# Sixteen more pairs in the layout of four chains, their values inside the y products

## The chip, the core and the metric

One core of a Trainium2 chip runs the whole program. The metric is the device time of one execution in microseconds. TensorE (PE in the rows) does the matmuls, VectorE (DVE) and ScalarE (ACT) the element-wise work and everything that leaves PSUM, GpSimd (POOL) some sums, SyncE (SP) issues the loads and stores.

## What is computed

The reference is windowed attention on 8 batches x 8 heads x 576 tokens x 64, followed by a feed-forward layer with a parametric ReLU on all 4608 tokens. Four heads of a batch see the last 32 tokens ("plain"), four see every fourth of the last 128 ("dilated").

```
scores = scale * np.matmul(q, k.transpose(0, 1, 3, 2))
mask_plain = (rel >= 0) & (rel < window)
mask_dil = (rel >= 0) & (rel < window * dilation) & (rel % dilation == 0)
...
attn = np.exp(scores)
attn = attn / (np.sum(attn, axis=-1, keepdims=True) + 1e-09)
return np.matmul(attn, v).astype(np.float32)
...
h = x @ w_in
g = np.maximum(h, 0.0) + alpha * np.minimum(h, 0.0)
return (g @ w_out).astype(np.float32)
```

x is the attention's output, 4608 x 512; w_in is 512 x 2048.

## The kernel before

Attention is done in 32 *pairs* of heads (8 batches x 4; class Pair; pair 4b + c). A dilated head is sorted by residue first, so that both kinds have a band of blocks: 32 queries against 64 keys. The steps of a pair are `scores` (PE; 36 small matmuls into two PSUM banks, each done as two passes, so 72 in the trace), `maxima` (DVE, four operations: mask and maximum), `exponentials` (ACT, nine), `divisions` (DVE, three), `turns` (DVE, one transpose of the probabilities from pr to pt), `values` (PE, from pt and v into PSUM tiles o), and `highs` and `lows`, which copy o to where the feed-forward layer or a store takes it. `keep` stores it.

Each large product is done as three passes on 128 x 128 weights and 512 columns (high x high, high x low, low x high). The work runs in 48 *slices*: slice n is one block f of 128 of the 2048 hidden units for one tile t of 512 tokens, tiles 0, 1 and 2. In slice n stand `ffn_h` of slice n + 1 (12 matmuls of 512 columns), the parametric ReLU (either `ffn_relu` on ACT and `ffn_sum` on DVE, or `ffn_parts`, two operations on DVE, in the slice after scores), `ffn_high` (ACT) and `ffn_low` (DVE), which split g in two parts, and `ffn_y` of slice n - 1 (12 matmuls into four y banks, column block by column block). Beside them stand preparations for the next stage: `combined_low` (wc) and `others_low` (ysum) on DVE with sums on GpSimd, and from slice 39 on parts of the next tiles. After the slices comes the *paired stage*, which does six tiles two at a time.

Pairs 0 to 7 stand at the start. Pairs 8 to 23 stand in slices 17 to 46. Pairs 24 to 31 stand in the paired stage, and these use the *layout of four chains* (`mixed`): a head is cut in chains of 5, 5, 4 and 4 blocks (`CHAINS`) in place of two halves of 9, v is laid out to fit (vX in place of vW), and the mask is another one. Values are then 42 matmuls on four o tiles, one for a chain; in the layout of halves 38 on two.

Every engine works in the order in which the code issues. PSUM has eight banks: four y banks, and four a banks that go round in turn (`bank("a", ...)`): each ffn_h takes the next one, scores of pairs 8 to 23 the next two, values the next two. A tile in a bank can be written when the reader of the bank's last tile is done.

`score_at`, `value_at` and `divide_at` say in which slice scores, values and divisions stand. Before, the values of a pair stand in the slice of the next pair's scores, right behind them. pr and pt exist once, so turns of a pair comes behind the values of the pair before it.

Of the kernel before, what the change touches and what calls it, by code (L numbers as in the profile page):

```python
# [66 lines left out]
def tile_window_attention_prelu_ffn(  # L67
# [127 lines left out]
    class Pair:  # L195
        def __init__(self, b, c):
            self.b, self.c = b, c
            p = b * NC + c
            self.onto = p <= NC + 1
            self.banks = "y" if self.onto else "a"  # L200
            self.late = p == 0
            self.plain = 2 * c < HP
            self.mask = PLAIN if self.plain else DILATED
            self.id = f"{b}_{c}"
            self.pr = spare_pr[p % 2] if b < 2 else pr0
            self.room = rooms[c] if b < 2 else None
            self.sm = sums[p % 2]
            self.mixed = p >= AHEAD
            self.kept = {}

        def target(self, t):

            if t not in KEPT:
                return half(t, self.c)
            if t not in self.kept:
                if self.mixed:
# [4 lines left out]
            return self.kept[t][0]  # L221

# [4 lines left out]
        def load_qk(self):  # L227
            b, c = self.b, self.c
            if self.mixed:
                self.k, self.q = lasting("k")[:, :S], lasting("q")[:, :S]  # L230
            elif self.room is None:
                self.k = att.tile([P, S], F32, tag="k", name=f"k_{self.id}")
                self.q = att.tile([P, S], F32, tag="q", name=f"q_{self.id}")
            else:
                self.k, self.q = self.room[:, :S], self.room[:, S:2 * S]
            nc.sync.dma_start(out=self.k, in_=kT[b, c])
            nc.sync.dma_start(out=self.q, in_=qT[b, c])

        def load_v(self):
            if self.mixed:  # L240
# [5 lines left out]
            nc.sync.dma_start(out=self.v, in_=vX[self.b - AHEAD // NC, self.c] if self.mixed else vW[self.b, self.c])  # L246

        def scores(self):


            if self.mixed:
# [91 lines left out]
        def turns(self):  # L343

            self.pt = lasting("pt") if self.mixed else att.tile([P, HB * BK], F32, tag="pt", name=f"pt_{self.id}")
            nc.vector.transpose(self.pt, self.pr.rearrange("q j k -> q (j k)"))
# [19 lines left out]
        def places(self):  # L366

            base = self.b * S
            if self.mixed:
                for n, (first, length) in enumerate(CHAINS):  # L370
                    a, last = first * BQ, (first + length) * BQ
                    flat = self.po[n].rearrange("d i q -> d (i q)")
                    while a < last:
                        if self.plain:
                            t = (base + a) // TT
                            z = min(last, (t + 1) * TT - base)
                            to = self.target(t)[:, base + a - t * TT:base + z - t * TT]
                        else:
# [4 lines left out]
                            to = self.target(t).rearrange("d (i r) -> d r i", r=DILATION)[:, r, i:i + z - a]  # L383
                        yield n % 2, flat[:, a - first * BQ:z - first * BQ], [to]
# [26 lines left out]
        def highs(self):  # L411
# [5 lines left out]
        def lows(self, copy=nc.vector.tensor_copy):  # L417
            for u, src, to in self.out:
                if len(to) == 2:
                    nc.vector.tensor_tensor(out=to[1], in0=src, in1=to[0].bitcast(F32), op=ALU.subtract)  # L420
                elif u == 1:
                    copy(out=to[0], in_=src)
# [105 lines left out]
    def ffn_y(t, f):  # L528
# [10 lines left out]
        for c in range(NC):  # L539
            for n, (a, e) in enumerate(PASSES):  # L540
# [3 lines left out]
                )  # L544

# [647 lines left out]
    def masks_of(kind):  # L1193
        nc.sync.dma_start(out=mask_sb[:, kind:kind + HB], in_=masks[:, kind:kind + HB])
# [97 lines left out]
    for n in range(CUT):  # L1292
# [16 lines left out]
        if scored:  # L1309
            scored.maxima()  # L1310
            if n == 0:
                behind(scored.nm, load, pairs[7].load_qk, pairs[7].load_v, lambda: masks_of(PLAIN))
# [42 lines left out]
    for n in range(CUT, NS):  # L1355
# [36 lines left out]
        if SECOND - 2 <= n < NS - 1:  # L1392
# [5 lines left out]
            ffn_high(*slices[n + 1])  # L1398
            if divided:
# [3 lines left out]
        if not whole:  # L1403
            ffn_y(*slices[n - 1])
# [7 lines left out]
        if valued:  # L1412
            valued.values()
            pairs[pairs.index(valued) + 1].load_v()
# [7 lines left out]
        if valued:  # L1422
            valued.highs()
            put[n + 1].append(valued.keep)
        if scored:
            scored.exponentials(5)
        if valued:
            valued.lows(nc.scalar.copy)
# [5 lines left out]
        if n == HALF + 1:  # L1434
            pairs[2 * NC].load_qk()
            pairs[2 * NC].load_v()
        if n in combine_at:
# [9 lines left out]
        if n == NS - 2:  # L1447
            nc.sync.dma_start(out=mask_sb, in_=masks[:, NMASK:2 * NMASK])
# [80 lines left out]
```

## Time and profile before

| | |
|---|---|
| median of 3 runs | 847.58 us (845.1 to 848.56) |
| profiled execution | 847.35 us |
| its span, first to last instruction | 845.6 us |
| PE busy | 825.9 us (98%) |
| DVE busy | 652.3 us (77%) |
| ACT busy | 466.3 us (55%) |
| granted TensorE clock | 0.996 of 2.4 GHz |

Busy times are sums over an engine's instructions with overlaps counted once; the difference of execution and span lies before the first and after the last instruction.

### The profile page before, as it was taken

Reading aid. Unit: us, or ns where it says so; the run is one execution under the profiler, and the core shown is the slowest. Engines: PE = TensorE matmul, PEld = TensorE weight load, DVE = VectorE, ACT = ScalarE, POOL = GpSimd, SP = SyncE. Lnnn points to the kernel's source line nnn. Section 1 sums busy time; section 2 is a strip of 40 time slices with the busy share of each in tenths; the row PEclk is TensorE's granted clock in tenths of the full one; section 3 lists DMA queues with packets and bytes.
Section 4 is the critical chain, followed back from the end, with each engine's and each line's share of the span. In section 5 each row is a group of like instructions: output and inputs, shape, how many; then the busy total and the mean of one; then the engine's idle time right before and its main releaser. Section 6 shows DMA issues by size and latency. Waiting matters only on the chain.

```text
span 845.6 us, 20392 instructions
## 1 busy us (share of the span) xinstructions
PE 825.9 (98%) x8014; PEld 671.3 (79%) x8014; DVE 652.3 (77%) x1087; ACT 466.3 (55%) x1276; POOL 87.0 (10%) x88
## 2 busy tenths in 40 slices
PE   8889999999999999999999999999999999999998
PEld 5677888878887887887888788878887888888886
DVE  5887767777668689879966999897289988944983
ACT  7785766735444555667436752665176436624640
POOL 0000000115575454000000000000000000000000
PEclk9999999999999999999999999999999999999999
DMA  7843389769776768595899599866876886666664
GB/s 255 277 160 126 125 255 276 250 210 280 250 251 222 266 213 286 193 302 168 266 311 303 156 326 298 260 183 201 252 208 196 288 286 198 192 194 190 197 191 157
DMA packets 131485, 194.90 MB, mean 230 GB/s; under 512 B 11582, under 2 KB 67518, under 8 KB 131390
## 3 DMA queue, kind: packets, MB, share of 16 engines
q1 hardware_dynamic: 131390, 193.60, 71.9%
q8 instruction: 63, 1.03, 0.5%
q14 instruction: 32, 0.26, 0.1%
HBM read 145.33 MB, written 48.23 MB: 229 GB/s over the span
## 4 chain that ended last, share of the span: by engine, by line
PE 81%; DVE 10%; ACT 4%; issue 2%; DMA 1%; SPq 0%; DVEq 0%; ACTq 0%
PE h L495 15%; PE qA L1027 15%; PE y L541 14%; PE pA L726 11%; PE qC L1027 7%; PE pC L726 6%; PE qB L1027 4%; PE o L361 3%; PE pB L726 3%; PE s L266 2%; DVE held L785 1%; ACT pr L331 1%; DVE stage L778 1%; DVE gp L840 1%; DVE py L956 1%
## 5 line engine op out<-in xcount | busy, mean ns | idle before, releaser
L495 PE MATMUL h<-x,w_dt.float32r 128*128 128x512 f32 x576 | 145.2, 401 | 3.3 <-DVE pr L318 1.2
L541 PE MATMUL y<-g,w_dt.float32r 128*128 128x512 f32 x576 | 138.3, 389 | 0.7 <-DVE ob L549 0.7
L495 PEld LDWEIGHTS h<-x,w_dt.float32r 128*128 128x128 f32 x576 | 108.6, 192 | 27.6 <-DVE pr L318 1.6
L541 PEld LDWEIGHTS y<-g,w_dt.float32r 128*128 128x128 f32 x576 | 108.0, 188 | 23.5 <-issue 1.1
L331 ACT ACTIVATE pr<-pr,nm 128x64 f32<-128x64 f32 x216 | 72.4, 338 | 25.7 <-DVE nm L321 25.4
L771 ACT COPY stage<-pA 128x512 f32<-128x512 f32 x72 | 42.2, 586 | 47.4 <-PE pA L726 46.5
L726 PE MATMUL pA<-parts_w,ring_w 128*128 128x512 f32 x234 | 58.2, 391 | 0.2 <-ACT stage L771 0.2
L835 ACT CAST gp<-held 128x512 fp32r<-128x512 f32 x60 | 37.2, 620 | 35.6 <-DVE held L831 35.4
L726 PE MATMUL pA<-parts_w,ring_xA 128*128 128x512 f32 x222 | 55.4, 393 | 0.7 <-ACT stage L771 0.7
L503 ACT ACTIVATE m<-h 128x512 f32<-128x512 f32 x33 | 19.7, 598 | 60.4 <-PE h L495 50.1
L726 PEld LDWEIGHTS pA<-parts_w,ring_w 128*128 128x128 f32 x234 | 43.6, 188 | 9.8 <-ACT stage L771 0.6
L526 DVE TENSOR_TENSOR g<-m,g 128x512 fp32r<-128x512 f32 x48 | 37.9, 789 | 15.5 <-ACT g L521 15.5
L726 PEld LDWEIGHTS pA<-parts_w,ring_xA 128*128 128x128 f32 x222 | 41.2, 188 | 10.5 <-ACT stage L771 1.9
L521 ACT CAST g<-m 128x512 fp32r<-128x512 f32 x48 | 29.7, 618 | 35.6 <-DVE m L508 18.1
L778 DVE TENSOR_TENSOR stage<-pC,stage 128x512 f32<-128x512 f32 x48 | 33.0, 688 | 13.4 <-ACT stage L771 8.3
L952 ACT COPY py<-qA 128x512 f32<-128x512 f32 x24 | 13.8, 588 | 52.0 <-PE qA L1027 51.2
L1027 PE MATMUL qA<-gp,ring_xA 128*128 128x512 f32 x174 | 42.3, 390 | 0.0
L840 DVE TENSOR_TENSOR gp<-held,gp 128x512 fp32r<-128x512 f32 x60 | 40.7, 686 | 1.6 <-ACT gp L835 1.6
L331 ACT ACTIVATION_READ_ACCUMULATOR pr<-pr,nm 128x1 f32 x216 | 40.9, 189 | 0.0
L956 DVE TENSOR_TENSOR py<-qC,py 128x512 f32<-128x512 f32 x24 | 16.0, 688 | 31.0 <-PE qC L1027 24.7
L1027 PE MATMUL qA<-gp,ring_w 128*128 128x512 f32 x162 | 39.5, 389 | 0.0
L1027 PEld LDWEIGHTS qA<-gp,ring_xA 128*128 128x128 f32 x174 | 32.5, 188 | 7.0 <-DVE gp L840 0.2
(188 smaller groups left out, 1702.7 us busy)
## 6 DMA issues: line engine op xcount, KB each, us to landing
ring_w<-wS SPq DMA_DIRECT2D x69, 256.0 KB, 3.2
ring_xA<-wS SPq DMA_DIRECT2D x66, 256.0 KB, 2.9
ring_xA<-wY SPq DMA_DIRECT2D x40, 256.0 KB, 3.8
ring_w<-wY SPq DMA_DIRECT2D x36, 256.0 KB, 3.5
ring_g<-wS SPq DMA_DIRECT2D x33, 256.0 KB, 3.0
wO<-w_dt.float32r SPq DMA_DIRECT2D x32, 256.0 KB, 4.3
wS<-wc SPq DMA_DIRECT2D x16, 512.0 KB, 4.3
ring_w<-wO SPq DMA_DIRECT2D x31, 256.0 KB, 3.3
```

Source lines behind the costliest of these rows:

```text
L331: nc.scalar.activation(out=self.pr[:, r, :], in_=self.ps[r // CUT0][:, r % CUT0, :] if self.onto else self.pr[:, r, :], func=AF.Exp, bias= ...
L361: nc.tensor.matmul(self.po[u][e * D:(e + 1) * D, a:z, :], lhsT=self.v[rows, i, :], rhs=self.pt[rows, a * BK + (BQ if i else 0):z * BK - (B ...
L495: nc.tensor.matmul(ms[t, f], lhsT=weight(0, a, f)[:, c * P:(c + 1) * P], rhs=half(t, c)[:, e, :], start=(c == 0 and n == 0), stop=(c == NC ...
L521: nc.scalar.copy(out=g[:, 0, :], in_=ms[t, f])
L526: nc.vector.tensor_tensor(out=g[:, 1, :], in0=ms.pop((t, f)), in1=g[:, 0, :].bitcast(F32), op=ALU.subtract)
L541: nc.tensor.matmul(ys[t][c], lhsT=weight(1, a, f)[:, c * P:(c + 1) * P], rhs=g[:, e, :], start=(first and n == 0), stop=(last and n == 2),)
L726: nc.tensor.matmul(to, lhsT=w[:, (2 * a + c) * P:(2 * a + c + 1) * P], rhs=part_of(name, e)[:, c * TT:(c + 1) * TT], start=start and c == ...
L771: nc.scalar.copy(out=self.s(n), in_=self.A)
L778: nc.vector.tensor_tensor(out=self.s(n), in0=getattr(self, src), in1=self.s(to), op=ALU.add)
L835: nc.scalar.copy(out=self.pair(n)[:, 0], in_=self.whole(n))
L840: nc.vector.tensor_tensor(out=p[:, 1], in0=self.whole(n), in1=p[:, 0].bitcast(F32), op=ALU.subtract)
L1027: nc.tensor.matmul(to(q)[c], lhsT=w[:, k * P:(k + 1) * P], rhs=rhs[:, e], start=(i, q) in firsts and n == 0, stop=i == GP - 1 and n == 2, ...
```

## The change

Pairs 8 to 23 take the layout of four chains too (`mixed` now from pair 8 on; `in_h` is what `mixed` was, the pairs of the paired stage). Their values take four a banks, one for a chain. They are issued from inside ffn_y, behind its third column block of four (`amid`), together with the load of the next v, all the copies on ACT (`highs(True)`) and the subtractions on DVE for the tokens of tile 2 (`lows(True)`). `values_at` is written out: one slice behind the next pair's scores for most pairs. From slice 20 on divisions, turns and ffn_low stand behind ffn_y. The two halves of the mask in the new layout are loaded earlier, one in the start-up, one in slice 9.

```
-            self.mixed = p >= AHEAD
+            self.mixed = p >= 2 * NC
+            self.in_h = p >= AHEAD
...
-                self.v = att.tile([P, HB + 1, D], F32, tag="v", name=f"v_{self.id}")
+                self.v = att.tile([P, HB + 1 + self.mixed, D], F32, tag="v", name=f"v_{self.id}")
...
-            self.po = [psp.tile([P, n, BQ], F32, tag=f"y{c}", name=f"o_{self.id}_{c}") for c, (_, n) in enumerate(CHAINS)]
+            self.po = [
+                psp.tile([P, n, BQ], F32, tag=f"y{c}", name=f"o_{self.id}_{c}") if self.in_h else
+                bank("a", [P, n, BQ], f"o_{self.id}_{c}") for c, (_, n) in enumerate(CHAINS)]
...
-                if len(to) == 2 or u == 0:
+                if len(to) == 2 or u == 0 or alone:
                     nc.scalar.copy(out=to[0], in_=src)
...
+            if amid and c == NC - 2:
+                amid()
...
-    turns_at = (17, 19, 21, 23, 25, 27, 29, 31, 33, 35, 37, 38, 40, 41, 43, 44, 46)
-    for p, (n, m) in enumerate(zip(turns_at, turns_at[1:]), 2 * NC):
-        score_at[n] = pairs[p]
-        value_at[max(m, 20)] = pairs[p]
+    turns_at = (17, 19, 21, 23, 25, 27, 29, 31, 33, 35, 37, 38, 40, 41, 43, 44)
+    values_at = (20, 22, 24, 26, 28, 30, 32, 34, 36, 38, 39, 40, 42, 44, 45, 46)
+    for p, (n, m) in enumerate(zip(turns_at, values_at), 2 * NC):
+        score_at[n], value_at[m] = pairs[p], pairs[p]
...
+        def amid():
+            valued.values()
+            pairs[pairs.index(valued) + 1].load_v()
+            valued.highs(True)
+            valued.lows(True)
+            put[n + 1].append(valued.keep)
+
+        if not whole:
+            ffn_y(*slices[n - 1], amid if valued else None)
+        if SECOND - 2 <= n < NS - 1:
             if divided:
                 divided.divisions()
                 divided.turns()
             ffn_low(*slices[n + 1])
-        if not whole:
-            ffn_y(*slices[n - 1])
...
         if scored:
             scored.scores()
             pairs[pairs.index(scored) + 1].load_qk()
-        if valued:
-            valued.values()
-            pairs[pairs.index(valued) + 1].load_v()
```

How that moves PE in slice 35 and the one behind it shows in two pieces. In the names of the rows h, y, g and m carry f and a running number, s and o the pair's place and the bank or chain, and the number behind that. First PE before the change, from the end of the y of slice 35 on:

```order
L541 MATMUL y_8_3_3393<-g_10_3387,w_2_dt.float32r 128x512 x3
L266 MATMUL s_1_0_3600<-k_1_3445,q_1_3446 32x64 x20
L266 MATMUL s_1_1_3601<-k_1_3445,q_1_3446 32x64 x16
L361 MATMUL o_0_1_3643<-pt_0_3544,v_0_3489 64x32 x2
L361 MATMUL o_0_0_3642<-pt_0_3544,v_0_3489 64x64 x2
```

The values o of pair 16 stand right behind the scores s of pair 17. After the change PE goes from the last scores of pair 17 into slice 36:

```order
L295 MATMUL s_1_0_3695<-k_1_3527,q_1_3528 32x64 x4
L503 MATMUL h_13_3754<-x_0_840,w_2_dt.float32r 128x512 x6
L503 MATMUL h_13_3754<-x_1_1121,w_2_dt.float32r 128x512 x6
L549 MATMUL y_8_0_3471<-g_11_3570,w_2_dt.float32r 128x512 x3
L549 MATMUL y_8_1_3472<-g_11_3570,w_2_dt.float32r 128x512 x3
L549 MATMUL y_8_2_3473<-g_11_3570,w_2_dt.float32r 128x512 x3
L315 MATMUL o_0_1_3782<-pt_0_3649,v_0_3627 64x32 x2
L315 MATMUL o_0_2_3783<-pt_0_3649,v_0_3627 64x32
L315 MATMUL o_0_3_3784<-pt_0_3649,v_0_3627 64x32
```

The values of pair 16 now come a slice later, behind three of the four y blocks, and o_0_3, the fourth chain, is among their first matmuls; its bank is that of h_13 above. The second place is DVE in slice 20, the first one with values. Before:

```order
L526 TENSOR_TENSOR g_14_2123<-m_14_2034,g_14_2123 128x512
L515 TENSOR_SCALAR m_15_2127<-h_15_2109,al 128x512
L516 SCALAR_TENSOR_TENSOR m_15_2127<-h_15_2109,m_15_2127 128x512
L338 TENSOR_SCALAR rs_1_2132<-sums_80 128x9
L339 RECIPROCAL rs_1_2132<-rs_1_2132 128x9
L340 TENSOR_TENSOR pr_78<-pr_78,rs_1_2132 128x576
L346 STREAM_TRANSPOSE pt_1_2136<-pr_78 128x576
```

After, with two rows that stay, the low part of the g before and the two operations of ffn_parts, and then the subtractions of `lows`:

```order
L534 TENSOR_TENSOR g_14_2124<-m_14_2035,g_14_2124 128x512
L523 TENSOR_SCALAR m_15_2128<-h_15_2110,al 128x512
L524 SCALAR_TENSOR_TENSOR m_15_2128<-h_15_2110,m_15_2128 128x512
L428 TENSOR_TENSOR x_0_840<-o_0_0_2142,x_0_840 128x160
L428 TENSOR_TENSOR x_0_840<-o_0_1_2143,x_0_840 128x160
L428 TENSOR_TENSOR x_0_840<-o_0_2_2144,x_0_840 128x64
L345 TENSOR_SCALAR rs_1_2202<-sums_80 128x9
```

The subtractions moved ahead of the divisions and turns of the next pair; what stands ahead of ffn_parts is unchanged.

## Rows read from the trace of the kernel before

**Rows 1.** Busy times of the stretch that holds slices 17 to 47.
```profile
core 0: us, PE busy (x) PEld busy (x) DVE busy (x) ACT busy (x) POOL busy (x), PEclk, DMA share, GB/s
147.00:362.00 215.00, 210.49 (x3104) 172.97 (x3103) 164.58 (x256) 115.53 (x424) 86.81 (x84) 1.00 0.75 242
```
**Rows 2.** Timeline of PE, slice 35: start, duration, instructions; scores (s), values between.
```profile
268.99 2.88 PE L495 MATMUL h<-x,w_dt.float32r 128*128 128x512 f32 x12
271.71 2.88 PE L541 MATMUL y<-g,w_dt.float32r 128*128 128x512 f32 x12
274.52 1.21 PE L266 MATMUL s<-k,q 64*32 64x64 f32 x72
...
276.94 3.02 PE L495 MATMUL h<-x,w_dt.float32r 128*128 128x512 f32 x12
279.80 2.88 PE L541 MATMUL y<-g,w_dt.float32r 128*128 128x512 f32 x12
```
**Rows 3.** Timeline of PE, slices 17 to 20: scores alone, then values alone.
```profile
147.62 2.88 PE L541 MATMUL y<-g,w_dt.float32r 128*128 128x512 f32 x12
...
154.44 2.88 PE L541 MATMUL y<-g,w_dt.float32r 128*128 128x512 f32 x12
...
162.69 1.21 PE L266 MATMUL s<-k,q 64*32 64x64 f32 x72
...
166.70 2.88 PE L541 MATMUL y<-g,w_dt.float32r 128*128 128x512 f32 x12
...
173.65 2.88 PE L541 MATMUL y<-g,w_dt.float32r 128*128 128x512 f32 x12
```
**Rows 4.** Timeline of PE, paired stage: scores, then values, in four chains.
```profile
362.06 1.52 PE L726 MATMUL pA<-parts_w,ring_w 128*128 128x512 f32 x6
363.51 0.97 PE L290 MATMUL s<-lasting_k,lasting_q 64*32 64x64 f32 x72
364.41 1.65 PE L726 MATMUL pC<-parts_w,ring_w 128*128 128x512 f32 x6
365.91 1.53 PE L726 MATMUL pA<-parts_w,ring_w 128*128 128x512 f32 x6
...
394.78 1.52 PE L726 MATMUL pC<-parts_w,ring_w 128*128 128x512 f32 x6
396.24 1.12 PE L308 MATMUL o<-lasting_pt,lasting_v 32*64 32x32 f32 x84
...
398.78 1.52 PE L726 MATMUL pA<-parts_w,ring_w 128*128 128x512 f32 x6
```
**Rows 5.** PE's groups, 176 to 357 us: busy, mean ns | idle before them, releasers.
```profile
L495 PE MATMUL h<-x,w_dt.float32r 128*128 128x512 f32 x300 | 74.3, 396 | 2.4 <-DVE pr L318 1.2 <-issue 1.2
L541 PE MATMUL y<-g,w_dt.float32r 128*128 128x512 f32 x305 | 73.6, 390 | 0.7 <-DVE ob L549 0.7
L361 PE MATMUL o<-pt,v 32*64 32x64 f32 (+1 forms) x1140 | 20.3, 218 | 1.5 <-DVE m L508 1.0 <-DVE pt L346 0.4
```
**Rows 6.** Timeline of DVE, slice 20: low part of g, then ffn_parts.
```profile
168.85 1.30 DVE L526 TENSOR_TENSOR g<-m,g 128x512 fp32r<-128x512 f32 x1 [1.64 <-ACT g L521]
170.08 0.74 DVE L515 TENSOR_SCALAR m<-h,al 128x512 f32<-128x512 f32 x1
170.85 0.69 DVE L516 SCALAR_TENSOR_TENSOR m<-h,m 128x512 f32<-128x512 f32 x1
```
**Rows 7.** Timeline of DVE, slice 29: first of maxima, others_low.
```profile
232.87 0.49 DVE L318 SCALAR_TENSOR_TENSOR pr<-s,mask_sb 128x320 f32<-128x320 f32 x1 [0.62 <-PE s L266]
...
235.71 1.22 DVE L628 TENSOR_TENSOR ysum<-ysum 128x1024 fp32r<-128x1024 f32 x1
```
**Rows 8.** Timeline of DVE, slices 40 and 41: first of maxima, ffn_parts, combined_low.
```profile
311.26 0.49 DVE L318 SCALAR_TENSOR_TENSOR pr<-s,mask_sb 128x320 f32<-128x320 f32 x1
...
315.91 0.75 DVE L515 TENSOR_SCALAR m<-h,al 128x512 f32<-128x512 f32 x1 [1.72 <-PE h L495]
...
322.44 1.22 DVE L604 TENSOR_TENSOR wc<-wsum_xA,wc 128x1024 fp32r<-128x1024 f32 x1
```
**Rows 9.** Timeline of ACT, paired stage: three copies out of o.
```profile
400.12 0.51 ACT L415 COPY between<-o 128x128 f32<-128x128 f32 x3
```

More of the change, by code (lines that the diff above doesn't have):

```diff
@@ L215, in target @@
             if t not in self.kept:
-                if self.mixed:
+                if self.in_h:
                     to = between(11 + 4 * (self.c & 1), len(self.kept))
@@ L221, in target, with sides @@
             return self.kept[t][0]
+        def sides(self, t):
+            x = self.target(t)
+            return [x[:, e] for e in range(2)] if t < NSTD else [x]
         def keep(self):
@@ L228, in load_qk @@
             b, c = self.b, self.c
-            if self.mixed:
+            if self.in_h:
                 self.k, self.q = lasting("k")[:, :S], lasting("q")[:, :S]
@@ L239, in load_v @@
         def load_v(self):
-            if self.mixed:
+            if self.in_h:
                 self.v = lasting("v").rearrange("p (j d) -> p j d", d=D)
             elif self.room is None:
-                self.v = att.tile([P, HB + 1, D], F32, tag="v", name=f"v_{self.id}")
+                self.v = att.tile([P, HB + 1 + self.mixed, D], F32, tag="v", name=f"v_{self.id}")
             else:
                 self.v = self.room[:, 2 * S:taken].rearrange("p (j d) -> p j d", d=D)
-            nc.sync.dma_start(out=self.v, in_=vX[self.b - AHEAD // NC, self.c] if self.mixed else vW[self.b, self.c])
+            nc.sync.dma_start(out=self.v, in_=vX[self.b - 2, self.c] if self.mixed else vW[self.b, self.c])
         def scores(self):
-            if self.mixed:
+            if self.in_h:
                 self.ps = [psp.tile([P, n, BK], F32, tag=f"y{2 + i}", name=f"s_{self.id}_{i}")
@@ L343, in turns @@
         def turns(self):
-            self.pt = lasting("pt") if self.mixed else att.tile([P, HB * BK], F32, tag="pt", name=f"pt_{self.id}")
+            self.pt = lasting("pt") if self.in_h else att.tile([P, HB * BK], F32, tag="pt", name=f"pt_{self.id}")
             nc.vector.transpose(self.pt, self.pr.rearrange("q j k -> q (j k)"))
@@ L376, in places @@
                             z = min(last, (t + 1) * TT - base)
-                            to = self.target(t)[:, base + a - t * TT:base + z - t * TT]
+                            cut = slice(base + a - t * TT, base + z - t * TT)
+                            to = [x[:, cut] for x in self.sides(t)]
                         else:
@@ L382, in places @@
                             i -= (t * TT - base) // DILATION
-                            to = self.target(t).rearrange("d (i r) -> d r i", r=DILATION)[:, r, i:i + z - a]
-                        yield n % 2, flat[:, a - first * BQ:z - first * BQ], [to]
+                            to = [x.rearrange("d (i r) -> d r i", r=DILATION)[:, r, i:i + z - a] for x in self.sides(t)]
+                        yield n % 2, flat[:, a - first * BQ:z - first * BQ], to
                         a = z
@@ L420, in lows @@
                     nc.vector.tensor_tensor(out=to[1], in0=src, in1=to[0].bitcast(F32), op=ALU.subtract)
-                elif u == 1:
-                    copy(out=to[0], in_=src)
+                elif u == 1 and not alone:
+                    nc.vector.tensor_copy(out=to[0], in_=src)
     staged, order = {}, {}
@@ L1191, in conversion, with masks_of @@
         return w
-    def masks_of(kind):
-        nc.sync.dma_start(out=mask_sb[:, kind:kind + HB], in_=masks[:, kind:kind + HB])
+    def masks_of(kind, base=0):
+        nc.sync.dma_start(out=mask_sb[:, kind:kind + HB], in_=masks[:, base + kind:base + kind + HB])
     def behind(t, *lots):
@@ L1311, in tile_window_attention_prelu_ffn @@
             if n == 0:
-                behind(scored.nm, load, pairs[7].load_qk, pairs[7].load_v, lambda: masks_of(PLAIN))
+                behind(scored.nm, load, pairs[7].load_qk, pairs[7].load_v, lambda: masks_of(PLAIN, NMASK))
             scored.exponentials(0, 5)
@@ L1421, in tile_window_attention_prelu_ffn @@
             ended.pop()()
-        if valued:
-            valued.highs()
-            put[n + 1].append(valued.keep)
         if scored:
             scored.exponentials(5)
-        if valued:
-            valued.lows(nc.scalar.copy)
         if n in split_at:
@@ L1508 @@
         np.stack([
-            v.reshape(B, NC, 2, 2 * HB, BQ, D)[AHEAD // NC:, :, chain(m, s)[0], max(0, CHAINS[chain(m, s)[1]][0] - 1 + i)]
+            v.reshape(B, NC, 2, 2 * HB, BQ, D)[2:, :, chain(m, s)[0], max(0, CHAINS[chain(m, s)[1]][0] - 1 + i)]
             for s in range(2) for i in range(CUT0 + 1 - s)], axis=3) for m in range(4)], axis=2)
```

9 lines of the change are left out of this document (4 added, 5 removed).

## The prediction

> **What bounds the kernel now.** The page comes first. TensorE (PE) is the busiest engine and the chain that ended last runs mostly through it, so the end moves by what PE gains or loses. Slices 17 to 47 hold all 16 pairs that the change touches; the busy times of that stretch [rows 1] show PE at work for 210.49 of 215.00 us, at full clock, with VectorE (DVE) at 164.58. So two things can move here: how long PE is busy, and its 4.5 us of gaps. The groups of PE's instructions, cut to that stretch, name the gaps [rows 5]: 1.2 us by no cause that the profile shows ("issue"), and 1.2 + 0.7 + 1.0 + 0.4 = 3.3 us for VectorE. DVE is not the bound, but it has work for three quarters of the time, in its own order, and PE waits wherever a bank is handed over late. That is the place to look.
>
> **What the insertion of a pair costs PE.** Twelve large matmuls take 2.72 us (268.99 to 271.71, [rows 2]). A slice that holds the scores of one pair and the values of another costs 279.80 - 271.71 - 5.44 = 2.65 us over its two products [rows 2]. Fourteen pairs stand so. Scores that stand alone cost 154.44 - 147.62 - 5.44 = 1.38 us, values alone 173.65 - 166.70 - 5.44 = 1.51 us [rows 3]; two of each stand so. In all 14 x 2.65 + 2 x 1.38 + 2 x 1.51 = 42.9 us.
>
> The layout of four chains isn't unknown to this trace: the eight last pairs use it in the paired stage, between large matmuls of the same kind. There scores cost 365.91 - 362.06 - 2.72 = 1.13 us, values 398.78 - 394.78 - 2.72 = 1.28 us [rows 4]. After the change every pair stands so: 16 x 2.41 = 38.6 us. The first term is **-4.3 us**. It already holds the price of standing apart: about 0.09 us of lead-in and 0.14 of run-out for each insertion (363.51 and 365.91 against 1.36 for six large matmuls), of which there are now 32 in place of 18.
>
> The Trainium skill, TensorEngine Tiling (Array Packing), section Tiling Modes, says that a change of tiling mode drains the engine. By that rule standing apart must cost; the rows agree (1.38 + 1.51 against 2.65), and give no reason for a higher price inside y than between two products.
>
> **The old waits.** The 3.3 us for VectorE have causes that the change takes away, all but one. Of the four banks in turn, h after the scores of a pair took that of its first scores, which maxima still reads (1.2); now h takes one that was emptied a slice ago. Values right behind the next scores waited on the sum of h or on turns (1.4); now turns of a pair is more than a slice old when its values come. The wait of y on ob (0.7) is a hand-over of the y banks; it stays, shorter (below). Second term: **-3.3 us**, with ob counted anew.
>
> **The new wait.** Values now take four banks. They rotate, h took the last turn, so chain 3 lands in the bank of the h of its own slice: the third bank that values touch, in their first few matmuls. PE may pass only when DVE has read that h (ffn_parts, two operations, 1.46 us from 170.08 to the end at 171.54 [rows 6]). Before, values took two banks and stopped short of it. To find who is late, put 0 at the start of a pair's scores. h starts at 0.90 [rows 4], y at 0.90 + 2.86 = 3.76 (276.94 to 279.80, [rows 2]), values behind three columns of y at 3.76 + 2.04 + 0.09 = 5.9. h can be read at about 4.0, so a free DVE is done by 5.5 and nobody waits. But ffn_parts stands behind the maxima of the scores and what follows them in DVE's order:
>
> Slice 20. DVE has still to do the low part of g, which waits 1.64 us for ScalarE, itself behind nine exponentials; it runs 1.30 us, and ffn_parts ends at 171.54 [rows 6]. The scores stood at 162.69 [rows 3], so this is at 8.85; all of that chain stays as it is. PE is there at 5.9: **+2.9 us**; 2.3 if g runs in half its time.
>
> Slice 30. Slice 29 has both a combined_low and an others_low behind the maxima; from the first of the maxima to the end of both are 235.71 + 1.22 - 232.87 = 4.06 us [rows 7]. The first starts when the mixed scores end, at 1.0 [rows 4], so ffn_parts ends at 6.5, and PE waits 0.65.
>
> Slice 42. The scores of pairs 20 and 21 come in neighbouring slices, after the change 0.90 + 2.86 + 2.72 + 0.09 = 6.6 us apart (8.1 before, with values between). DVE's work from the first maxima to the end of combined_low is 322.44 + 1.22 - 311.26, less 1.72 in which it waits for h: 10.7 us [rows 8]. With 1.0 ahead and ffn_parts behind, it is done at 13.1 - 6.6 = 6.6, and PE waits 0.7.
>
> The same sum gives 0.2 at slice 32, 1.1 at 34 (ob and an others_low come late there), 0.1 at 39, 0.65 at 44 and 0.8 at 45 (parts of the next stage stand in DVE's way); the other eight are 0, within 0.1. Together with 30 and 42 **+4.2 us**. From below it is 0, from above 1.3 us at each of these seven, what the longer forms of the same operations (1.30 us for a 0.69 us g [rows 6]) would add: 9 us. I take the middle since DVE's chains are continuous where PE is late.
>
> **Emptying the banks.** The next h takes chain 0's bank, 0.8 us after the values' end (three matmuls of y and the run-out). ScalarE copies four to eleven pieces; three short ones go by within 0.51 us [rows 9], so chain 0 is out in time, and most slices with values have no exponentials of their own in the way. Only in the four pairs of batch 2 DVE must subtract too: 0.3 us at the two dilated ones. Scores behind values in one slice (38, 40, 44) want chains 0 and 1: 0.2. With 0.4 left of the wait on ob, this is **+1.2 us**: 0 if all is out in time, 4 if ob keeps its 0.7 and chain 0 holds h up by 0.4 in each of the eight dilated pairs.
>
> Free are: the mask in two loads ahead of time, since SyncE's queue has no one waiting there; v, a tenth larger, loaded a slice ahead; turns behind the values of the pair before, at 7.0 on the same clock, when the division is done anyway; more and smaller ScalarE copies, in slices without exponentials.
>
> Sum: -4.3 - 3.3 + 2.9 + 4.2 + 1.2 = +0.7 us, against the profiled execution's 847.35 us, which stands 0.2 us under the median of the runs shown: **848.2 us**. Less than 0.5% (4.2 us) can't be told from no change here.
>
> **The rivals.**
> *The new wait shows at slice 20 alone* (DVE finds room everywhere else, since PE's own stalls give it time). For it speaks that DVE is idle for 50 us of the stretch; against it that the late places are chains without gaps. 847.35 - 7.6 + 2.9 + 0.4 = 843.0 us, and 840 if slice 20 also costs less.
> *VectorE falls behind in most value slices*: ffn_parts ends at 7.1 and later in slices 30 to 45, through longer forms or a POOL operation beside them, so that each of the seven late slices pays 1.3 us. It decides from about 1.1 us a slice on, where the seven sum up to 7.6, all that the change saves. 9 us in place of 4.2, and chain 0 late as well, 2 us: 848.2 + 4.9 + 2 = 855 us. The Trainium skill, TensorEngine Tiling (Array Packing), section Restrictions and Gotchas, speaks for it: row tiling raises the pressure on PSUM, as different row tiles write to different banks. This trace shows so much of it that values on two banks waited 1.0 us for one [rows 5].
> *The layout brings nothing inside the slices*: scores and values cost what they cost alone now, 16 x 2.89 = 46.2 us. Then 848.2 + 7.6 = 856 us; against it stands that the neighbours in the paired stage are the same 512-column matmuls.
>
> **How the numbers follow.** The forecast, the gain eaten by the new wait, 0.53: 844.5 to 852 us. The first rival 0.25, the second 0.17, the third 0.05. The range reaches from most of the first rival to a part of the second: 841.5 to 853.5. Faster by over 0.5% (under 843.1) holds most of the first rival and a little of the forecast's edge, 0.25; slower (over 851.6) both of the others and as little of the edge, 0.23; the rest 0.52.
>
> **What would show it.** In the profile after: PE's idle time before L315 (values) put down to DVE m of ffn_parts, some 7 us in all, near 3 of it once, at 168 to 171 us; no wait of h on pr; scores at about 0.97 us and values at 1.12 us a pair in the slices. If the wait at slice 20 is under 2 us, or the sum of the others under 2 or over 8, the middle was wrong; if scores keep 1.21 us, the first term was.

## The result, and the profile after

The changed kernel takes 851.74 us (median of 10 runs, 847.81 to 855.95), the kernel before 847.02 us beside it; the ratio is 1.0059, with a 95% interval of 1.0034 to 1.0084. So it is about 0.6% slower, just past what can be told from no change. The forecast of 848.2 us lies 3.5 us below, its range holds the time. The profiled execution took 851.13 us, its span 849.0 us.

The span alone misleads here: the start-up, which is the same in most kernels below, ends anywhere from 147.3 to 152.5 us. So every kernel is also read by its **stretch**, from the start of the first scores of pair 8 to the first pA of the paired stage (150.44 to 362.06 before, the end in [rows 4]): 211.62 us before, 365.41 - 150.60 = 214.81 us after, 3.2 us more.

First the groups of PE's instructions after, 147 to 366 us, as in [rows 5]: busy us, mean ns, then idle time and its releasers.

```profile
L549 PE MATMUL y<-g,w_dt.float32r 128*128 128x512 f32 x384 | 96.9, 396 | 0.1
L503 PE MATMUL h<-x,w_dt.float32r 128*128 128x512 f32 x353 | 89.3, 402 | 3.1 <-issue 2.8 <-ACT x L423 0.2
L315 PE MATMUL o<-pt,v 32*64 32x64 f32 (+1 forms) x1344 | 19.7, 231 | 5.0 <-DVE m L524 5.0
L295 PE MATMUL s<-k,q 64*32 64x64 f32 x1152 | 15.5, 224 | 0.0
```

The old waits on pr, pt and the sum are gone. In their place values wait 5.0 us on DVE m of L524, which is ffn_parts, and h waits 2.8 us for "issue", no cause that the profile names; before, "issue" was 1.2. Where this is, the timeline of PE after shows (start, duration; first scores, slices 20, 22, 24, 30, 34, 40 and 41, 44, 45, start of the paired stage):

```profile
150.60 0.97 PE L295 MATMUL s<-k,q 64*32 64x64 f32 x72
...
168.53 0.31 PE L315 MATMUL o<-pt,v 32*64 32x32 f32 x6
171.61 1.05 PE L315 MATMUL o<-pt,v 32*64 32x32 f32 x78 [2.77 <-DVE m L524]
172.59 0.98 PE L549 MATMUL y<-g,w_dt.float32r 128*128 128x512 f32 x3
...
176.24 2.88 PE L549 MATMUL y<-g,w_dt.float32r 128*128 128x512 f32 x12
179.05 0.97 PE L295 MATMUL s<-k,q 64*32 64x64 f32 x72
179.95 3.02 PE L503 MATMUL h<-x,w_dt.float32r 128*128 128x512 f32 x12
182.81 2.20 PE L549 MATMUL y<-g,w_dt.float32r 128*128 128x512 f32 x9
184.94 1.13 PE L315 MATMUL o<-pt,v 32*64 32x32 f32 x84
186.00 0.97 PE L549 MATMUL y<-g,w_dt.float32r 128*128 128x512 f32 x3
186.80 2.98 PE L503 MATMUL h<-x,w_dt.float32r 128*128 128x512 f32 x12
...
198.95 1.05 PE L315 MATMUL o<-pt,v 32*64 32x32 f32 x78 [0.26 <-DVE m L524]
...
240.22 1.05 PE L315 MATMUL o<-pt,v 32*64 32x32 f32 x78 [0.32 <-DVE m L524]
...
268.46 1.05 PE L315 MATMUL o<-pt,v 32*64 32x32 f32 x78 [0.67 <-DVE m L524]
...
309.79 1.12 PE L315 MATMUL o<-pt,v 32*64 32x32 f32 x84
...
311.74 0.97 PE L295 MATMUL s<-k,q 64*32 64x64 f32 x72
312.64 0.50 PE L503 MATMUL h<-x,w_dt.float32r 128*128 128x512 f32 x1
315.97 4.06 PE L503 MATMUL h<-x,w_dt.float32r 128*128 128x512 f32 x11 [2.83 <-issue]
319.83 3.15 PE L549 MATMUL y<-g,w_dt.float32r 128*128 128x512 f32 x12
322.91 0.97 PE L295 MATMUL s<-k,q 64*32 64x64 f32 x72
...
343.06 1.05 PE L315 MATMUL o<-pt,v 32*64 32x32 f32 x78 [0.65 <-DVE m L524]
...
351.45 1.05 PE L315 MATMUL o<-pt,v 32*64 32x32 f32 x78 [0.35 <-DVE m L524]
...
365.41 1.52 PE L736 MATMUL pA<-parts_w,ring_w 128*128 128x512 f32 x6
```

Slice 20 is as forecast: six matmuls of the values, then 2.77 us of wait. A slice where nobody waits (22) costs what the sum said: scores 182.81 - 176.24 - 5.44 = 1.13 us, values 186.80 - 182.81 - 2.72 = 1.27 us, against 1.13 and 1.28 in [rows 4]. Slice 41 is new: one matmul of h, 2.83 us of nothing, and then eleven matmuls in 4.06 us that take 2.65 us at full clock (the same eleven in a run below). The windows of that place show the clock, PEclk being the granted clock as a share of 2.4 GHz:

```profile
core 0: us, PE busy (x), PEclk, DMA share, GB/s
312.00:316.00 4.00, 1.17 (x70) 1.00 0.94 262
316.00:320.00 4.00, 4.00 (x12) 0.62 0.55 195
320.00:325.00 5.00, 5.00 (x90) 0.96 0.06 6
```

The stall cost its own 2.83 us and behind it a stretch in which the clock stood at its lower level (1.2 GHz) for most of the time. What arrives in the stall is seen in the DMA queues between 313.50 and 313.75 us (packets, MB, share of the 16 engines):

```profile
q1 hardware_dynamic: 36, 0.10, 98.2%
q8 instruction: 1, 0.02, 24.0%
```

That packet on the instruction queue is taken here for a piece of PE's program (the count that bears this out stands with e5 and e6), and PE goes on some 2.3 us later. The same order, a q8 packet and PE's return 2.2 to 2.4 us behind it, stands at the gap of 1.19 us before (packet at 178.5, return at 180.81) and at each gap of this kind in the runs below.

### The profile page after: what moved, and what is told of

It is laid out like the page before. It is cut to its first block, busy times and chain, and to the rows that moved or that the text cites. A ratio compares the mean times of both kernels' runs of the same rounds, so it can differ in the third digit from the quotient of the medians.

```text
span 849.0 us, 20753 instructions
## 1 busy us (share of the span) xinstructions
PE 825.0 (97%) x8142; PEld 665.0 (78%) x8142; DVE 657.4 (77%) x1099; ACT 472.1 (56%) x1346; POOL 90.0 (11%) x88
## 4 chain that ended last, share of the span: by engine, by line
PE 77%; DVE 14%; ACT 5%; issue 2%; DMA 2%; SPq 0%; DVEq 0%; ACTq 0%
PE qA L1037 15%; PE h L503 13%; PE y L549 13%; PE pA L736 11%; PE qC L1037 7%; PE pC L736 5%; PE qB L1037 4%; PE o L315 3%; PE pB L736 3%; ACT pr L338 2%; PE s L295 2%; DVE held L795 1%; PE o L368 1%; DVE pr L325 1%; DVE nm L328 1%
## 5 line engine op out<-in xcount | busy, mean ns | idle before, releaser
L503 PE MATMUL h<-x,w_dt.float32r 128*128 128x512 f32 x576 | 146.9, 405 | 4.0 <-issue 2.8
L549 PE MATMUL y<-g,w_dt.float32r 128*128 128x512 f32 x576 | 143.0, 394 | 0.1
```

The lines of the kernel that those rows point to most:

```text
L503: nc.tensor.matmul(ms[t, f], lhsT=weight(0, a, f)[:, c * P:(c + 1) * P], rhs=half(t, c)[:, e, :], start=(c == 0 and n == 0), stop=(c == NC ...
L549: nc.tensor.matmul(ys[t][c], lhsT=weight(1, a, f)[:, c * P:(c + 1) * P], rhs=g[:, e, :], start=(first and n == 0), stop=(last and n == 2),)
```

## The experiments

All times stand against the kernel before, run beside it. For each kernel: ratio, stretch of the profiled execution (one profile each), and in it PE's waits on DVE and by "issue", and whether the clock fell. Waits on ACT (most in e8) and on a load (e7) stand in the text.

| kernel | ratio [95%] | stretch | DVE | issue | clock fell |
|---|---|---|---|---|---|
| before | 1 | 211.62 | 3.3 | 1.2 | no |
| after | 1.0059 [1.0034, 1.0084] | 214.81 | 5.0 | 2.8 | at 316 |
| e1 parts first | 1.0031 [1.0013, 1.0049] | 211.85 | 4.3 | 2.1 | no |
| e2 code shift | 1.0129 [1.0105, 1.0152] | 212.20 | 7.2 | 0 | no |
| e3 halves amid | 0.9999 [0.9982, 1.0015] | 210.06 | 0.4 | 0 | no |
| e4 values later | 1.0015 [0.9997, 1.0032] | 212.72 | 6.1 | 0 | at 168 |
| e5 load later | 1.0048 [1.0030, 1.0067] | 215.35 | 6.0 | 2.0 | at 318 |
| e6 more traffic | 1.0091 [1.0073, 1.0109] | 217.15 | 7.4 | 2.0 | at 314 |
| e7 all | 1.0033 [1.0009, 1.0057] | 213.71 | 2.5 | 0 | at 300 |
| e8 behind y | 1.0067 [1.0049, 1.0086] | 217.25 | 3.5 | 0.8 | at 168 |
| e9 two moves | 0.9972 [0.9955, 0.9989] | 210.06 | 4.7 | 0 | no |
| e10 some later | 0.9958 [0.9940, 0.9977] | 209.06 | 4.1 | 0 | no |
| e11 and weights | 0.9968 [0.9948, 0.9987] | 208.55 | 3.9 | 0 | no |

The theory after the result: the layout saves what was said; the wait on ffn_parts takes most of it back; the rest is a gap in which PE waits for its program, and the clock behind it. The rivals: the gap belongs to the work of slice 41, or to the transfers; the wait is not worth its size; the place amid y is what costs.

**The wait at slice 20 (e1).** Only DVE's order changes: the low part of g waits for ScalarE behind ffn_parts, no longer ahead of it.

```
-            ffn_low(*slices[n])
+            if n < SECOND - 2:
+                ffn_low(*slices[n])
...
             ffn_high(*slices[n + 1])
+            if n == SECOND - 2:
+                ffn_low(*slices[n])
```

> The kernel after, with the low part of g of slice 20 put behind ffn_parts in DVE's order. Theory: the wait of 2.77 us before the values of slice 20 is DVE's own order, and nothing else holds PE there, so ffn_parts ends 2.9 us earlier, the wait falls under 0.3 us, and the time by 2.8 us, from 851.7 to about 848.9 us. Rival: the wait takes time that PE would lose a little later anyway (on g, or on the division's end before the next values); then the idle time moves to slices 21 to 22, and the time stays within 1 us of 851.7. PE's instructions are the same, so the gap of 2.8 us by no named cause at slice 41 stays about where it is.

Timeline of PE in that kernel, slices 20 and 41:

```profile
169.22 0.31 PE L315 MATMUL o<-pt,v 32*64 32x32 f32 x6
170.62 1.05 PE L315 MATMUL o<-pt,v 32*64 32x32 f32 x78 [1.09 <-DVE m L524]
...
314.86 2.65 PE L503 MATMUL h<-x,w_dt.float32r 128*128 128x512 f32 x11 [2.06 <-issue]
```

The wait falls by 1.7 us, not by 2.8: the low part of a weight (L484, 1.58 us in DVE's timeline) still stands ahead of ffn_parts, which the expectation had overlooked. No wait comes up in slices 21 to 23, so the rival falls there. Later y waits 0.61 us on ob and the values of slice 44 wait 1.01 in place of 0.65; the wait on ob stands in e5 and e6 too (0.61 and 0.60), where slice 20 is as after. The gap stands at the same place, behind the 4159th matmul of the program, is 0.8 us shorter and without the low clock. The ratio goes from 1.0059 to 1.0031, 2.4 us, near the 2.8 expected; but only 1.7 of it is the wait; the rest may be the gap's and the clock's.

**Where PE stands in its program (e2, e4).** e2 adds 32 small matmuls on zeros in slice 0, so that every later matmul stands 64 places further on (two passes each). e4 moves the values of pair 19 from slice 40 to 41, so that they and the scores of pair 20 no longer stand together.

```
+        if n == 0:
+            idle("y0", 32, BQ)
```

> The kernel after, with 32 small matmuls on zeros (32 columns each) added in slice 0, where PE waits for the attention; nothing else is touched. They move every later place of PE's program by 32 matmuls against the data transfers. Theory: the gap of 2.8 us at slice 41, put down to issue, is PE waiting for a piece of its own program that comes late through full DMA queues, so it depends on where a piece ends; moved by 32 matmuls, it goes to another place, shrinks or disappears, and with it the lower clock behind it: 847.5 to 850 us, 851.7 if it lands as badly elsewhere. Rival: the gap belongs to the work of slice 41 (a semaphore or queue that the profile does not name); then it stays at the h behind the scores of slice 40, 2.8 us long, and the time stays at 851.7, plus up to 2 us if the added matmuls are not hidden.

```
-    values_at = (20, 22, 24, 26, 28, 30, 32, 34, 36, 38, 39, 40, 42, 44, 45, 46)
+    values_at = (20, 22, 24, 26, 28, 30, 32, 34, 36, 38, 39, 41, 42, 44, 45, 46)
...
-                reload(t, c)
+                if n == 41 and c == 3:
+                    put[n + 1].append(lambda t=t, c=c: reload(t, c))
+                else:
+                    reload(t, c)
```

> The kernel after, with the values of pair 19 in slice 41 in place of slice 40 (their store of tile 4 and its reload one slice later too), so that no scores stand right behind values there and the load of the next v goes out a slice later. Theory: in slice 40 values and scores together use up PE's program fastest (156 small matmuls with their weight loads in some 3.5 us) while the transfers are at their limit; apart, the piece of the program comes in time, the gap of 2.8 us at slice 41 and the low clock behind it are gone, and the time falls by about 4 us to 847.5 to 848.5 us. Rival: the gap has nothing to do with either; then it stays at the first h behind slice 40, and the time within 1 us of 851.7.

In both the gap is gone, nowhere else in the stretch is there one, and the clock is full at that place. In e2 slice 41 is untouched, so its work isn't the cause. The added matmuls weren't hidden: with others of their kind they form one block of PE's timeline, at the clock's lower level, and the first scores of pair 8 start at 157.64 us in place of 150.60:

```profile
39.77 11.96 PE L127 MATMUL idle<-pr 128*128 128x512 f32 x66
```

The late start is most of what e2 loses: 7.2 us against before, of the 7.8 by which its profiled execution (855.11 us) is longer. The other four executions took 855.48 to 858.87 us, at mean clocks of 0.989 to 0.992 against 0.994, so the ratio of 1.0129 holds more than the profile shows. Its stretch is 2.6 us shorter than after. e4's ratio is 1.0015, but its profile shows the clock fall at another place, behind the wait of slice 20 (timeline, then windows):

```profile
168.51 1.05 PE L315 MATMUL o<-pt,v 32*64 32x32 f32 x78 [2.75 <-DVE m L524]
169.49 1.63 PE L549 MATMUL y<-g,w_dt.float32r 128*128 128x512 f32 x3
170.92 3.88 PE L503 MATMUL h<-x,w_dt.float32r 128*128 128x512 f32 x12
```

```profile
168.00:172.00 4.00, 3.49 (x84) 0.69 0.34 91
172.00:176.00 4.00, 4.00 (x17) 0.88 0.73 222
```

Three matmuls of y take 1.43 us to the next start in place of 0.81, twelve of h 3.71 in place of 2.84: 1.5 us for a stall that after, e2, e5 and e6 had too (2.76 to 2.77 us) without that.

**The transfers (e5, e6).** e5 issues the v load of slice 40 a slice later, e6 the 1 MB store at the start of slice 40 twice; PE's program is untouched in both.

```
-            pairs[pairs.index(valued) + 1].load_v()
+            if n == 40:
+                put[n + 1].append(pairs[pairs.index(valued) + 1].load_v)
+            else:
+                pairs[pairs.index(valued) + 1].load_v()
```

> The kernel after with one load moved: the v load (352 KB) that goes out in slice 40, just behind the 1 MB store of ysum, goes out a slice later. PE's program is the same, matmul for matmul. Theory: the gap at slice 41 is a piece of PE's program that arrives late behind full queues; with 352 KB less ahead of it (some 0.95 us at the 370 GB/s of that stretch), the gap shrinks from 2.83 to about 1.9 us or less, and the lower clock behind it does not come: 2 to 4 us less than after, ratio to before 1.001 to 1.004. Rival: the gap comes from where PE stands in its program alone; then it stays 2.8 us, and the ratio at 1.006.

```
             put[n + 1].append(lambda i=cast_at[n]: others_store(i))
+            if n == 39:
+                put[n + 1].append(lambda i=cast_at[n]: others_store(i))
```

> The kernel after with the suspected cause doubled: the 1 MB store of ysum at the start of slice 40 is issued twice (same data, same place). PE's program is the same. Theory: the piece of the program waits for the queues, so the gap at slice 41 grows, by up to 2.8 us (1 MB at 370 GB/s), with the lower clock behind it; the ratio to before goes from 1.006 to about 1.009. k and q of pair 21, loaded behind the store, come later too; a wait of scores on k or q would show by its name in the trace and is counted apart. Rival: transfers have no part in it; the gap stays 2.8 us and the ratio at 1.006.

e5's gap is 2.03 us, near the expected 1.9, but e1, whose loads are as after, has 2.06, so the moved load isn't shown to be the reason. The clock falls all the same, and the ratio of 1.0048 is 0.9 us under after, where 2 to 4 were expected; the two intervals overlap. e6's gap is shorter than after, not longer: 2.01 us, with the low clock. Timeline of PE, and the queues around the packet of the program (311.75 to 312.00 us):

```profile
311.68 0.50 PE L503 MATMUL h<-x,w_dt.float32r 128*128 128x512 f32 x1
314.19 4.26 PE L503 MATMUL h<-x,w_dt.float32r 128*128 128x512 f32 x11 [2.01 <-issue]
```

```profile
q8 instruction: 1, 0.02, 23.7%
q1 hardware_dynamic: 3, 0.00, 4.5%
```

My theory that the packet comes late through full queues falls as its cause: here the queues are all but empty (SyncE's queue was held up by the doubled store, and the loads behind it went out later), and the gap is there. What stays: PE runs out of program at this matmul, whatever is being moved, for 2.01 to 2.06 us in three of the five kernels that have the place. After's extra 0.8 us, with 36 other packets in the same quarter of a microsecond, may be the queues', and was seen once; e1's packet stands among 29 others (79.8%) without it. e6's 1.0091 comes from elsewhere: waits on m are up at slices 39, 42 and 44 (0.44, 1.00 and 1.10 us, against 0, 0 and 0.65 after), so its time was forecast for the wrong reason.

A count over the traces shows why it is this matmul. Of PE's records (matmuls, weight loads and PE's own semaphore and drain records) 8385 stand ahead of the gap in after, e1, e5, e6 and e8, and 4289 in the kernel before: 4096 fewer, which is 16 x 256. The 13 traces have 63 to 65 packets of 16 KB on q8 for 16,317 to 16,705 records, so one packet for 256 records, and a gap stands where one such piece ends. With the records cut at these ends and the packets taken in order, none of the 823 pieces in these traces is begun sooner than 2.2 us behind its packet. The piece ahead of the gap is nearly all small matmuls, the values of pair 19 and the scores of pair 20 with their weight loads (247 of 256 records): after, PE went through it in 2.62 us, where the next shortest piece of the stretch took 6.25; in e4, which puts the two apart, the shortest takes 6.25. e2's 64 more matmuls and 64 weight loads move the ends by half a piece. A short piece alone is not enough: in the stretch five others of 1.95 to 2.78 us (three before, one each in e2 and e3) passed without a stop, as the next packet had come 0.8 to 3.1 us ahead of their start; at the gaps it came 1.4 to 3.5 us behind it.

**The place and the layout apart (e3, e8).** e3 keeps the new places and goes back to halves for pairs 8 to 23. e8 keeps the layout and puts values behind all of y.

```
-            self.mixed = p >= 2 * NC
+            self.mixed = p >= AHEAD
```

> The kernel after with pairs 8 to 23 back in the layout of halves (mixed from pair 24 on, masks loaded as before); the places of values, highs, lows and divisions stay as in the kernel after. Theory: each pair costs 1.38 + 1.51 = 2.89 us alone, 46.2 us in all against 42.9 before (+3.3); the old waits are gone (-3.3), and two banks do not reach the h of the same slice, so no wait on ffn_parts appears: 847 to 848 us, the same as the kernel before within 1 us, but for gaps by no named cause. Rival: the layout is worth nothing in the slices, or the place amid y is the expensive part: then this kernel costs as much as the kernel after or more, 851 us and up, with scores and values of a pair no longer than after by 0.48 us.

Groups of PE in e3, its stretch:

```profile
L549 PE MATMUL y<-g,w_dt.float32r 128*128 128x512 f32 x375 | 94.5, 395 | 0.4 <-DVE ob L559 0.4
L503 PE MATMUL h<-x,w_dt.float32r 128*128 128x512 f32 x348 | 86.0, 396 | 0.0
L368 PE MATMUL o<-pt,v 32*64 32x64 f32 (+1 forms) x1216 | 21.7, 218 | 0.0
L271 PE MATMUL s<-k,q 64*32 64x64 f32 x1152 | 19.3, 217 | 0.0
```

All waits but 0.4 us are gone: the new places take away the old waits by themselves, and two banks bring no new one. The stretch is 1.6 us shorter than before, of which 1.2 is the old gap; the time is the same. Less 720 large matmuls (163.2 us) and waits, scores and values cost 46.5 us in e3 (46.2 forecast for halves alone) and 42.0 in the kernel of e9, which has four chains and the same places but for pair 19 and the low part of g in slice 20: the layout saves 4.5 us there. The line of values in e9, 147 to 361 us (y waits 0.6 on ob besides):

```profile
L315 PE MATMUL o<-pt,v 32*64 32x64 f32 (+1 forms) x1344 | 19.9, 231 | 4.1 <-DVE m L524 4.1
```

```
-            if amid and c == NC - 2:
+            if amid and c == NC - 1:
```

> The kernel after with values behind all four column blocks of y in place of three: 0.68 us later for the bank of h, and 0.68 us less between the end of values and the next h, which takes chain 0's bank. Theory: the waits on ffn_parts shrink by 0.68 us each (slice 20 to 2.1, slices 24, 30, 44 and 45 to nothing: 2.3 us less in all), and the emptying of the banks comes into the open: 0.5 to 0.8 us before the next h in each of the 16 slices with values, 8 to 12 us in all, so 5 to 10 us slower than after, ratio 1.012 to 1.017. Rival: ScalarE empties chain 0 in time in either place; then this kernel is 2 us faster than after, ratio 1.003.

Groups of PE in e8, 147 to 365 us:

```profile
L503 PE MATMUL h<-x,w_dt.float32r 128*128 128x512 f32 x348 | 89.6, 406 | 7.7 <-ACT kept L423 3.4 <-ACT x L423 2.1 <-DVE x L428 1.4
L315 PE MATMUL o<-pt,v 32*64 32x64 f32 (+1 forms) x1344 | 18.7, 231 | 2.1 <-DVE m L524 2.1
L295 PE MATMUL s<-k,q 64*32 64x64 f32 x1152 | 16.0, 224 | 1.4 <-ACT kept L423 1.4
```

Both mechanisms are as expected: slice 20 at 2.1 us and no other wait on m, 2.9 us less; and the emptying of the banks in the open, 14 waits of 0.34 to 1.04 us, 8.3 us in all (12 on ScalarE's copies, two on DVE's subtractions). These two make 5 us more, as forecast; but the gap, at the same matmul, is 0.84 us in place of 2.83, the stretch is 2.4 us longer, and by time e8 (1.0067) can't be told from after (1.0059), a miss for its 1.012 to 1.017. The three blocks of y ahead of values hide the readers of h, the one behind hides the copies; neither of the two places hides both.

**Moving the waits on (e7, e9 to e11).** e9 is e1 and e4 together. e7 adds to it that the low parts of wc and ysum that stand behind the maxima go behind ffn_low of the next slice, wherever that has values, and the weight's low part behind ffn_parts in slice 20; e10 does so for three slices and without the weight, e11 with it. In e7 the low part of one combined weight is taken from another's sums; the amount of work is the same.

```
+    def soon(n, op):
+        if n in (23, 29, 33):
+            later[n + 1].append(op)
+        else:
+            op()
...
             ffn_low(*slices[n + 1])
+        for op in later.pop(n, ()):
+            op()
...
-            combined_low(split_at[n])
+            soon(n, lambda i=split_at[n]: combined_low(i))
```

> The kernel after with every wait that was found moved out of the way: in slice 20 ffn_parts ahead of the low parts of g and of the last weights; values of pair 19 in slice 41; combined_low and others_low that stood behind the maxima put behind ffn_low of the next slice when that slice has values (their stores a slice later). Theory: the waits on ffn_parts (5.0 us) fall under 1 us in all, no gap at slice 41, no stall of PE long enough for the clock to fall; the stretch from the first scores of pair 8 to the paired stage takes 205.5 to 207 us against 211.6 before and 214.8 after, the time is 841 to 842.5 us, ratio to before 0.993 to 0.996. Rival: DVE only pushes its lateness on, to divisions and turns and so to the next values, or to the stores that feed the paired stage; then the waits come back as pt or ring waits, and the ratio is 1.000 or more.

(The piece of code is e10's.) In e7 the waits on m nearly go, and the rival holds: a wait of 2.58 us comes up at the scores of slice 38, and one of 1.46 at those of slice 44, this time for a load. PE's timeline and SyncE's queue in e7:

```profile
299.64 0.99 PE L295 MATMUL s<-k,q 64*32 64x64 f32 x72 [2.58 <-DMA q<-qT]
```

```profile
285.54 0.93 SPq L619 DMA_DIRECT2D wS<-wc  x2
...
289.81 0.98 SPq L642 DMA_DIRECT2D wY<-ysum  x1
290.88 0.51 SPq L241 DMA_DIRECT2D k<-kT  x1
291.44 0.92 SPq L242 DMA_DIRECT2D q<-qT  x1
```

The two stores of wc (1 MB) now go out just ahead of the 1 MB of ysum, and k and q stand behind both. The clock falls once more behind that stall (0.63 at 300 to 304 us).

> The kernel after with two moves together: ffn_parts ahead of the low part of g in slice 20, and the values of pair 19 in slice 41. Theory: both gains add, since one is DVE's order and the other the place where PE runs dry of program: the stretch from the first scores of pair 8 to the paired stage takes 214.8 - 4.4 (gap and low clock) - 1.7 (slice 20) = 208.7 us and up to 1 us more for waits that the gap hid, against 211.6 before; ratio to before 0.997 to 1.000. Rival: the gap only sits at a place of its own in the program and shows again elsewhere; ratio 1.002 to 1.004.

> The kernel of the two moves, with combined_low and others_low of slices 23, 29 and 33 alone put behind ffn_low of the next slice, and their stores one slice later, where no scores follow closely. Theory: the waits on ffn_parts at slices 24, 30 and 34 (0.26 + 0.32 + 0.67 us) and three stops of PE inside the values (about 0.23 us of emptying and filling each) go: 2 us less than the two moves alone, ratio 0.995 to 0.998. Rival: the stores that come later collide with the loads of k and q as they did when all were deferred; then a wait of scores on q or k appears at slice 25, 31 or 35 and after, and the ratio is no better than with the two moves.

> As the kernel before it, and in slice 20 the low part of the last converted weights behind ffn_parts as well. Theory: ffn_parts of slice 20 ends another 1.5 us earlier, the last 1.1 us of wait at slice 20 and its stop of PE go, and PE has no stall over 1.1 us in the stretch: 1.3 us less, ratio 0.993 to 0.997. Rival: the weights are then late for a product of slices 21 to 22, and the wait comes back there under the name of the weight.

e9 gives 0.9972, in its forecast range, with no gap; its stretch of 210.06 us is 0.4 over the top of what was expected. e10 gives 0.9958, the waits of slices 24 and 30 are gone and that of slice 34 is 0.31 us, and no load is late; 1.0 us less in the stretch, half of what was expected: a wait of 0.30 us came up at slice 32, and that of y on ob grew from 0.6 to 1.0 us. e11 has the shortest stretch, 208.55 us, and no wait in the values of slice 20; but 0.82 us of the gain is lost at once to a wait of h on DVE (x, L428), so that 0.5 us less came where 1.3 were expected. By time e9, e10 and e11 can't be told from each other; all three are faster than both kernels, e10 by 0.4% and 1.0%.

## Why the prediction was right in its range and 3.5 us short

**Right.** The price of scores and values in the new layout, to 0.01 us each where nobody waits (slice 22). The old waits: gone. The place and the size of the new wait at slice 20 (2.77 for 2.9), and its cause in DVE's order, though only 1.7 us of it is the low part of g, which the prediction named, and the last 1.1 the low part of a weight (gone in e11). Of the late slices that were named, 30, 34, 44 and 45 wait; 32, 39 and 42 don't, and 24, which was put at nothing, does. That no h waits on pr. The third rival (the layout brings nothing) falls by the rows of slice 22; the first (slice 20 alone) and the second (1.3 us in each late slice) both fall by the five waits of 0.26 to 0.67 us.

**Mis-sized: the same wait at the later slices.** The sum had 4.2 us for them; the rows show 0.26 + 0.32 + 0.67 + 0.65 + 0.35 = 2.25 us. Slice 42 shows nothing after, where the gap stands ahead of it; without the gap it waits 1.02 us (e2). But each wait costs more than its idle time: the values that stop take 0.31 + 0.98 us of PE, those that don't 1.06 (168.53 to 172.59 less 2.77, against 184.94 to 186.00), so 0.23 us for the stop of slice 20. At that price six stops are 1.4 us. With slice 20, 6.4 us in place of 7.1. The Trainium skill, TensorEngine Tiling (Array Packing), section Tiling Modes, has the engine drained by a change of mode, not of the tile alone; these rows have one mode on both sides of the stop, which all the same costs 0.23 us beyond its wait.

**Not settled: emptying the banks.** 1.2 us in the sum. After, what is left of the stretch when the large matmuls (163.2), scores and values at 2.41 us a pair (38.6), the stops and waits (6.4), the gap (2.8) and the low clock (some 1.8 at the rows of 312.64 to 322.91) are taken out is 2.0 us, ob with it. Only 0.3 us of that shows as a wait (ACT x L423 0.2, y 0.1), so that the rest is the banks' isn't shown; before has 1.0 us of the same kind. e8 shows how thin the cover is.

**Failed: "1.2 us by no cause that the profile shows", taken as unchanged.** That term was carried over as if it belonged to the kernel. It belongs to where a piece of PE's program ends and how fast PE comes to that end: 1.19 us at one place before, 2.83 at another after, none in e2 to e4. With the low clock behind it, which the sum did not have at all, this is 2.83 - 1.19 + 1.8 = 3.4 us, more than the whole difference between +0.7 and the 3.2 us of the stretch; the smaller errors go against each other (the new waits -0.7, the rest put down to the banks +0.8, and before's own scores and values 43.9 in place of 42.9, which makes the change -1.0). That the sum came as near as 2.5 us is in part luck of these errors. With pair 19 moved and the gap gone by it, e4 stands at 1.0015, where +0.7 us would be 1.0008; with slice 20 mended as well, e9 is faster than before.

The balance by experiment: places alone (e3) 210.06 us, places and layout without gap (e9) 210.06 us. What the layout saves, 4.5 us, is what its waits on DVE cost, 4.7 - 0.4 = 4.3 us: the forecast's main statement, seen with both kernels free of gaps, in one profile each and with slice 20 mended in e9. By ratio e9 stands lower, 0.9972 against 0.9999, with intervals that overlap.

**Open.** What sets off the packet of a piece, which comes anywhere from 3.7 us ahead of the start of the piece before it to 7.5 us behind in these stretches, and whether full queues gave the extra 0.8 us. Why the clock fell behind stalls of 2.01, 2.03, 2.10, 2.58, 2.75 and 2.83 us and not behind others of 2.06, 2.76 and 2.77: no run separates them. The scatter of the changed kernel goes with the clock: its runs with a mean clock of 0.999 took 847.81 and 849.89 us, one with 0.990 855.95 us.

## What to carry to other kernels

Take a hand-over of banks as a loan: more banks for one user means that the next one waits for a reader that nobody waited for, and the engine that empties it must be early, not only fast. An idle gap "by no cause" is no constant: look in the queues for a packet of the program beside it, and expect it to move with any change in the number or order of instructions, above all where two groups of small matmuls stand close; compare stretches of equal work, not spans. When work is moved behind another engine's, follow the stores that hang on it, and what stands behind these in the queue.

## What the runs showed of the hardware

PE's program comes in pieces while the kernel runs: 64 packets of 16 KB on the instruction queue in one execution of after, one for 256 of PE's records, and PE stands still when one isn't there: 0.84 to 2.83 us at this place, with the queues all but empty at 0.84, 2.01 and 2.03. The Trainium skill, Trainium Architecture — The Big Picture, section The software stack, has the instruction streams moved to the engines when the program is loaded; here packets of the instruction queue arrive all through the execution, and at the six gaps PE's return follows its packet by 2.2 to 2.4 us.

A stall of PE of 2.0 to 2.8 us was followed in six profiles by 4 us at a granted clock of 0.60 to 0.78, 1.5 us of loss in e4 and 1.8 after, and in others of the same length by none. So a stall of this size can cost more than it shows.
